# A second v piece transposed by DMA instead of on TensorE, with later weights, a closer softmax and a lagging last chunk

## The chip, the cores and the metric

The kernel runs on one core of one Trainium2 chip. The metric is the device time of one execution in microseconds. Runs agree to some 0.3%, so what is at stake here, a microsecond in 571, lies at the edge of what times alone can show. Much of the argument is therefore read from the traces, where a gap of 0.1 us on TensorE can be seen. "Clock" below means the kernel's own agenda clock, by which the program decides at build time what is emitted between which matmuls; it starts at the first main matmul of each batch, and in the first batch it is about 37.3 us behind the span's time.

In the profiles PE is TensorE (matmuls), ACT ScalarE and DVE VectorE (casts, products, copies), POOL GpSimd (it issues the loads), SP SyncE (it issues the DMA transposes and most stores); a "q" behind an engine's name is its instruction queue. A DMA "lands" when its data are all there. Batches and, by number, chunks and pieces count from 0: the second v piece of batch 0 is piece 1 in the code.

## The reference, cut to what matters

```python
# attention over channels, B, N, C = 4, 5824, 256
qn = q / (norm(q, axis=1) + 1e-6);  kn = k / (norm(k, axis=1) + 1e-6)
a = softmax(kn.transpose(0, 2, 1) @ qn / tau)          # one 256 x 256 matrix per batch
x = (v @ a).reshape(B * N, C)                          # 23296 tokens
# feed-forward, d_ff = 1024
out = ((x @ w1) * (x @ w2)) @ w3 @ w_out
```

The kernel folds the small matrix `a` into `w1` and `w2` once per batch (the folds), and `w3 @ w_out` into one matrix once for all (the w units). What is left per batch is v, transposed, times two folded weights (`a` and `b` in the profile), their product (`abs`), and that times the folded output weight (`o`).

## The kernel before

A batch has 12 chunks of 8 steps. A step is four 512-column matmuls for `a` and `b`, then a cast on ACT and a product on DVE; the output matmuls of earlier products follow. The twelfth chunk is short (192 columns). Beside batch b, the scores and the softmax of batch b + 1 run. The moves, that is, the loads, have times on the clock, and two brakes on GpSimd's queue: a `gate` copies one element of the latest product, so a load does not start early; a `hold` copies one element of a transposed v piece, so the loads behind it start only when that transpose has landed.

```python
def gate():
    if last_ab[0] is not None:
        nc.gpsimd.tensor_copy(gate_t, last_ab[0][:1, :1])
def hold(src):
    nc.gpsimd.tensor_copy(gate_t, src)
...                                                    # (cut) first batch
    moves = [("qk", 1, 0, 29.0), ("v", 0, 3, 30.0), ("v", 0, 4, 30.5), ("qk", 1, 1, 44.0), ("qk", 1, 2, 45.0)]
    moves += [("qk", 1, 3, 53.0), ("qk", 1, 4, 55.0), ("v", 0, 5, 61.0), ("qk", 1, 5, 73.0)]
    moves += [("v", 1, 0, 88.0), ("v", 1, 1, 98.0), ("v", 1, 2, 120.0), ("qk", 2, 0, 130.0)]
    t0, t1 = 54.0, 113.0                               # window of batch 1's scores
...
before = (0, 2) if b == 0 else None
for nm, m, pi, t in moves:
    if before is not None and not (nm == "v" and before == (m, pi - 1) == (0, 3)):
        at(t, 0.0, hold of the transposed piece `before`)         # (shortened)
    at(t, 0.0, gate)
    if nm == "qk":
        at(t, 0.0, lambda m=m, pi=pi: load_qk(m, pi))
        before = None                                  # behind a q/k load no hold
    else:
        at(t, 0.0, lambda m=m, pi=pi: load_piece("v", m, pi))
        at(t + 4.0, 0.0, lambda m=m, pi=pi: transpose_piece(m, pi))   # DMA transpose, SP's queue
        before = (m, pi)
```

The outputs pass through three buffers (`o_sb`, copied by ACT and DVE from PSUM, the memory that matmuls write to).

## Time and profile before

| | |
|---|---|
| time, median of all six runs taken beside the changed kernel | 571.32 us (570.57 to 572.03) |
| span of the profiled run | 569.5 us |
| first main matmul, last matmul start | 37.26, 565.36 us |
| from the last matmul's start to the end | 4.10 us |
| TensorE busy | 558.9 us (98%) |

The main lines of this profile are shown in the prediction below. Three more views matter later. The first is GpSimd's timeline, with start, duration, what it does, and in brackets the idle time before it and what ended it:

```profile
101.84 0.52 POOL L109 DMA_DIRECT2D v<-in_v_dram  x1 [0.27 <-issue]
123.52 0.18 POOL L469 COPY gate_t<-vTt 1x1 bf16<-1x1 bf16 x1 [20.60 <-DMA vTt<-v]
125.87 0.56 POOL L112 DMA_DIRECT2D k<-in_k_dram  x1
```

The sixth v piece is issued at 101.84, the hold for its transposes ends at 123.52, and the last k of batch 1 goes out behind that, at 125.87. It landed at 134.3 us. TensorE at the end of batch 2, with batch 3's exponentials in progress:

```profile
428.13 0.60 PE L519 MATMUL o<-W_sb,abs 128*128 128x256 bf16 x4
428.78 0.59 PE L477 MATMUL a<-vT,Wf 128*128 128x512 bf16 x2
```

Four 256-column matmuls need 0.44 us from start to start; here it is 0.65.

### The profile page before, as it was taken

How to read it: one execution, taken by the hardware profiler on the slowest of the kernel's cores; microseconds unless marked ns; L12 is line 12 of the kernel's file. 1: busy time of each engine (PE TensorE's matmuls, PEld its weight loads, DVE VectorE, ACT ScalarE, POOL GpSimd, SP SyncE). 2: the span in 40 equal slices, each digit the busy share in tenths (PEclk: the TensorE clock that was granted, in tenths of full speed). 3: DMA queues.
4: the chain of work that ended last, by engine and by line, in shares of the span. 5: the costliest groups of instructions: out<-in, count | busy, mean ns of one | idle time of the engine just before them, and what ended most of it. 6: DMA issues, size and time to landing. Idle time of an engine off the chain costs nothing.

```text
span 569.5 us, 10098 instructions
## 1 busy us (share of the span) xinstructions
PE 558.9 (98%) x3755; PEld 354.9 (62%) x3755; DVE 375.7 (66%) x581; ACT 340.5 (60%) x627; POOL 77.2 (14%) x163
## 2 busy tenths in 40 slices
PE   8799999999999999999999999999999999999997
PEld 5664576776666666666666666666665656656665
DVE  1047645788966577887766567787866665565564
ACT  1057535777766577777675567777756554454453
POOL 4260013020220110121210111030120000000000
PEclk9999999999999999999999999999999999999999
DMA  9999989978455696595761495766740325221011
GB/s 213 211 175 208 168 170 233 225 171 195 112 147 120 132 194 147 98 184 128 148 148 73 95 217 121 155 120 121 184 112 39 85 74 148 63 70 68 38 73 58
DMA packets 75105, 77.45 MB, mean 136 GB/s; under 512 B 54193, under 2 KB 58801, under 8 KB 75057
## 3 DMA queue, kind: packets, MB, share of 16 engines
q0 software_dynamic: 15760, 38.93, 39.1%
q1 hardware_dynamic: 59072, 37.69, 22.3%
q8 instruction: 29, 0.48, 0.3%
q10 hardware_dynamic: 224, 0.20, 0.1%
q14 instruction: 20, 0.16, 0.1%
HBM read 78.91 MB, written 23.86 MB: 180 GB/s over the span
## 4 chain that ended last, share of the span: by engine, by line
PE 91%; DMA 6%; ACT 1%; DVE 1%; POOL 0%; issue 0%; ACTq 0%; POOLq 0%
PE o L519 28%; PE b L477 27%; PE a L477 27%; PE G L193 5%; DMA k<-in_k_dram 5%; PE fold L364 2%; DMA w3T<-w_wout 1%; PE w L643 1%; ACT kr L284 0%; ACT as L483 0%; PE quarter L390 0%; POOL k L112 0%; DVE s L318 0%; ACT e L323 0%; DVE abs L498 0%
## 5 line engine op out<-in xcount | busy, mean ns | idle before, releaser
L498 DVE TENSOR_TENSOR abs<-as,b 128x512 bf16<-128x512 bf16 x336 | 230.2, 686 | 138.0 <-ACT as L483 124.9
L483 ACT CAST as<-a 128x512 bf16<-128x512 f32 (+1 forms) x384 | 216.2, 563 | 173.4 <-DVE abs L498 87.1
L477 PEld LDWEIGHTS <-Wf 128*128 128x128 bf16 x1536 | 148.8, 98 | 101.7 <-issue 1.8
L477 PE MATMUL a<-vT,Wf 128*128 128x512 bf16 x704 | 209.4, 379 | 0.4 <-ACT Wf L399 0.4
L477 PE MATMUL b<-vT,Wf 128*128 128x512 bf16 x704 | 209.4, 379 | 0.0
L519 PE MATMUL o<-W_sb,abs 128*128 128x256 bf16 x1344 | 201.1, 273 | 0.0
L519 PEld LDWEIGHTS <-abs 128*128 128x128 bf16 x1344 | 131.4, 98 | 80.8
L202 DVE TENSOR_TENSOR acc<-acc,sq 128x1024 f32<-128x1024 f32 x66 | 80.4, 1219 | 0.7 <-ACT sq L190 0.7
L193 PE MATMUL G<-k,q 128*128 128x256 bf16 x276 | 49.6, 273 | 0.0
L190 ACT ACTIVATE sq<-q 128x512 f32<-128x512 bf16 x66 | 41.8, 634 | 0.0
L190 ACT ACTIVATE sq<-k 128x512 f32<-128x512 bf16 x66 | 41.6, 630 | 0.0
L465 POOL COPY gate_t<-abs 1x1 bf16<-1x1 bf16 x39 | 9.4, 241 | 170.1 <-DVE abs L498 168.8
L540 DVE COPY osb<-o 128x512 f32<-128x512 f32 x44 | 30.1, 684 | 0.9 <-PE o L519 0.9
L193 PEld LDWEIGHTS <-q 128*128 128x128 bf16 x276 | 27.0, 98 | 3.1
L539 ACT COPY osb<-o 128x512 f32<-128x512 f32 x44 | 25.8, 586 | 3.8 <-PE o L519 1.8
L469 POOL COPY gate_t<-vT 1x1 bf16<-1x1 bf16 x16 | 3.3, 208 | 162.5 <-DMA vT<-v 162.5
L112 POOL DMA_DIRECT2D q<-in_q_dram x28 | 15.1, 539 | 12.5 <-DMA k<-in_k_dram 5.5
L284 ACT ACTIVATE kr<-row 128x256 f32<-128x256 f32 x1 | 0.4, 384 | 26.0 <-PE row L272 26.0
L371 ACT ACTIVATE Wf<-fold,rs 128x512 bf16<-128x512 f32 x15 | 10.3, 688 | 9.0 <-PE fold L364 9.0
L488 DVE TENSOR_TENSOR left<-as,b 128x192 bf16<-128x192 bf16 x32 | 11.2, 353 | 5.7 <-ACT as L483 3.5
L364 PE MATMUL fold<-w,e 128*128 128x512 bf16 x56 | 14.7, 379 | 0.0
L498 DVE TENSOR_TENSOR abq<-as,b 128x512 bf16<-128x512 bf16 x16 | 10.8, 686 | 5.1 <-ACT as L483 4.6
(98 smaller groups left out, 241.8 us busy)
## 6 DMA issues: line engine op xcount, KB each, us to landing
out_dram<-osb SPq DMA_DIRECT2D x44, 512.0 KB, 3.6
k<-in_k_dram POOLq DMA_DIRECT2D x19, 512.0 KB, 8.6
v<-in_v_dram POOLq DMA_DIRECT2D x19, 512.0 KB, 5.2
q<-in_q_dram POOLq DMA_DIRECT2D x18, 512.0 KB, 6.6
w_wout<-in_moe_w_dram POOLq DMA_DIRECT2D x1, 2048.0 KB, 23.1
k<-in_k_dram POOLq DMA_DIRECT2D x4, 320.0 KB, 7.6
v<-in_v_dram POOLq DMA_DIRECT2D x4, 320.0 KB, 5.3
q<-in_q_dram POOLq DMA_DIRECT2D x3, 320.0 KB, 4.3
```

The lines of the kernel that those rows point to most:

```text
L112: nc.gpsimd.dma_start(out=pieces[nm, n, pi][:, lo:hi, :], in_=qk_main[nm, n][0][:, pi * PIECE + lo : pi * PIECE + hi, :])
L190: nc.scalar.activation(out=dst[:, :, part, :], in_=src[:, o : o + 2, :], func=AF.Square)
L193: nc.tensor.matmul(G[:, ct, :], lhsT=qt[:, i, ct * P : (ct + 1) * P], rhs=kt[:, i, :], start=(pr == 0 and part == 0 and ct == 0), stop=(pr ...
L202: nc.vector.tensor_add(accs[n], accs[n], sqs[0])
L364: nc.tensor.matmul(m, lhsT=st["e"][:, c2, c1 * P : (c1 + 1) * P], rhs=w12[:, c2, w, lo:hi], start=(c2 == 0), stop=(c2 == CT - 1),)
L477: nc.tensor.matmul(t[:, :n], lhsT=Wf[b][:, ct, w, j * P : (j + 1) * P], rhs=rhs_of(b, c, ct), start=(ct == 0), stop=(ct == CT - 1),)
L483: nc.scalar.copy(a_sb[:, :n], tiles[0][:, :n])
L488: nc.vector.tensor_mul(both, a_sb[:, :n], tiles[1][:, :n])
L498: nc.vector.tensor_mul(ab, a_sb, tiles[1])
L519: nc.tensor.matmul(tl[h][:, o, :], lhsT=lhsT, rhs=W_sb[:, j, :], start=(j == 0 and o == 0), stop=(j == FT - 1 and (small or o == 1)), skip ...
L539: nc.scalar.copy(o[:, 0:2, :], tl[0])
L540: nc.vector.tensor_copy(o[:, 2:4, :], tl[1])
```

## The change

Its intent: sixteen PE transposes less on the bounding engine, by sending the second v piece through the DMA transpose; w3 and w_out out of its way; fewer waits at batch ends and at the program's end.

```diff
-            [(0.0, 0.0, norms), (0.0, 6.0, k_row)]
-            + [(0.0, 6.0 + 1.3 * i, lambda i=i: k_step(i)) for i in range(4)]
... (softmax units, each with closer times)
-            + [(0.2, 16.5, sums)]
-            + [(0.43, 17.5 + 1.1 * i, lambda i=i: fold(i)) for i in range(8)]
+            [(0.0, 0.0, norms), (0.0, 5.5, k_row)]
+            + [(0.0, 5.5 + 1.2 * i, lambda i=i: k_step(i)) for i in range(4)]
+            + [(0.2, 14.6, sums)]
+            + [(0.43, 15.6 + 1.1 * i, lambda i=i: fold(i)) for i in range(8)]
...
-            at(7.0, 0.5, lambda: transpose_half_on_pe(0, 1, 0, True))
-            at(8.0, 0.5, lambda: transpose_half_on_pe(0, 1, 1, False))
-            at(15.0, 0.0, transpose_w3)
-            at(15.0, 0.0, lambda: transpose_piece(0, 2))
+            at(0.0, 0.0, lambda: transpose_piece(0, 2))
+            at(0.0, 0.0, lambda: transpose_piece(0, 1))
+            at(0.0, 0.0, lambda: hold(vTs[0][0][:1, PIECE, 0, :1]))
+            at(0.0, 0.0, load_w3)
+            at(16.0, 0.0, transpose_w3)
-                at(26.0 + 1.2 * jt, 0.87, lambda jt=jt: w_unit(jt))
-            moves = [... as above ...]
+                at(35.0 + 1.2 * jt, 0.87, lambda jt=jt: w_unit(jt))
+            moves = [("qk", 1, 0, 35.0), ("v", 0, 3, 35.5), ("qk", 1, 1, 49.0), ("qk", 1, 2, 51.0), ("qk", 1, 3, 55.0)]
+            moves += [("v", 0, 4, 58.0), ("qk", 1, 4, 68.0), ("v", 0, 5, 69.0), ("qk", 1, 5, 84.0)]
+            moves += [("v", 1, 0, 92.0), ("v", 1, 1, 102.0), ("v", 1, 2, 120.0), ("qk", 2, 0, 130.0)]
+            t0, t1 = 55.0, 113.5
-        before = (0, 2) if b == 0 else None
+        before = "w3" if b == 0 else None      # hold for the last w3 transpose
...
-                lag = LAG_END if b == B - 1 and c == NCH - 1 else LAG
+                lag = LAG
+                if b == B - 1 and c >= NCH - 2:
+                    lag = LAG_END if c == NCH - 1 else LAG + (LAG_END - LAG) * (j + 1) // FT
-    while pend:
-        emit_out(*pend.pop(0))
+    n = len(pend)
+    for i, only in [(i, 1) for i in range(n - 1)] + [(i, 0) for i in range(n - 2)] + [(n - 1, 1), (n - 2, 0), (n - 1, 0)]:
+        emit_out(*pend[i], only=only)
```

In the last lines `only=1` are the leftover rows of a batch pair, `only=0` the last ordinary rows. The two stores of the leftover rows now both leave from SP; before, one left from SP and one from ACT.

More of the change, by code (lines that the diff above doesn't have):

```diff
@@ L419, in soft_units @@
         return (
-            [(0.0, 0.0, norms), (0.0, 6.0, k_row)]
-            + [(0.0, 6.0 + 1.3 * i, lambda i=i: k_step(i)) for i in range(4)]
-            + [(0.0, 6.5, q_sums), (0.0, 9.3, lambda: q_norm(st["ss"]))]
-            + [(0.0, 11.3 + 1.3 * ct, lambda ct=ct: scale(ct)) for ct in range(CT)]
-            + [(0.0, 12.0 + 1.3 * ct, lambda ct=ct: exps(ct)) for ct in range(CT)]
-            + [(0.2, 16.5, sums)]
-            + [(0.43, 17.5 + 1.1 * i, lambda i=i: fold(i)) for i in range(8)]
+            [(0.0, 0.0, norms), (0.0, 5.5, k_row)]
+            + [(0.0, 5.5 + 1.2 * i, lambda i=i: k_step(i)) for i in range(4)]
+            + [(0.0, 6.0, q_sums), (0.0, 8.5, lambda: q_norm(st["ss"]))]
+            + [(0.0, 10.3 + 1.2 * ct, lambda ct=ct: scale(ct)) for ct in range(CT)]
+            + [(0.0, 11.0 + 1.2 * ct, lambda ct=ct: exps(ct)) for ct in range(CT)]
+            + [(0.2, 14.6, sums)]
+            + [(0.43, 15.6 + 1.1 * i, lambda i=i: fold(i)) for i in range(8)]
         )
@@ L501, in emit_ab, with emit_out @@
         clock[0] += 4 * (n * MM_COL + MM_FIX)
-    def emit_out(b, c, j, ab):
+    def emit_out(b, c, j, ab, only=None):
         small = c == NCH - 1
@@ L517, in emit_out @@
         for s, lhsT in reversed(list(enumerate(lhs))) if small else enumerate(lhs):
+            if only is not None and s != only:
+                continue
             h, o = (s, 0) if small else divmod(s, 2)
@@ L528, in emit_out @@
             if small:
-                nc.scalar.copy(o[:, 0, :], tl[0][:, 0, :])
-                other = nc.scalar if b == B - 1 else nc.sync
-                other.dma_start(out=rows[:, NT - 1, :], in_=o[:, 0, :])
-                if b % 2 == 1:
+                if b % 2 == 1 and only != 0:
                     o2 = work.tile([P, D], F32, tag="kr", name=f"oleft_{b}", bufs=1)
                     nc.vector.tensor_copy(o2, tl[1][:, 0, :])
-                    for k, eng in enumerate((nc.sync, other)):
-                        m = b - 1 + k
-                        eng.dma_start(out=out[m * N + NT * P : (m + 1) * N, :], in_=o2[k * LEFT : (k + 1) * LEFT, :])
+                    for m in (b - 1, b):
+                        k = (m - b + 1) * LEFT
+                        nc.sync.dma_start(out=out[m * N + NT * P : (m + 1) * N, :], in_=o2[k : k + LEFT, :])
+                if only != 1:
+                    nc.scalar.copy(o[:, 0, :], tl[0][:, 0, :])
+                    other = nc.scalar if b == B - 1 else nc.sync
+                    other.dma_start(out=rows[:, NT - 1, :], in_=o[:, 0, :])
             else:
@@ L541, in emit_out @@
                 nc.sync.dma_start(out=rows[:, 4 * c : 4 * c + 4, :], in_=o)
-            del out_tiles[b, c]
+            if only is None:
+                del out_tiles[b, c]
     NDEF = 4
@@ L615 @@
     load_piece("v", 0, 2)
-    nc.gpsimd.dma_start(out=wout_sb, in_=moe_w_out.rearrange("(lh ll) c -> ll lh c", ll=P))
-    nc.gpsimd.dma_start(out=w3_bf, in_=w3r)
     squares("k", 4, whole)
@@ L652, in w_unit, with load_w3 @@
             w_ready[0] = True
+    def load_w3():
+        nc.gpsimd.dma_start(out=wout_sb, in_=moe_w_out.rearrange("(lh ll) c -> ll lh c", ll=P))
+        nc.gpsimd.dma_start(out=w3_bf, in_=w3r)
     def load_library():
@@ L669, in make_agenda @@
             at(4.6, 0.5, lambda: transpose_half_on_pe(0, 0, 1, False))
-            at(7.0, 0.5, lambda: transpose_half_on_pe(0, 1, 0, True))
-            at(8.0, 0.5, lambda: transpose_half_on_pe(0, 1, 1, False))
-            at(15.0, 0.0, transpose_w3)
-            at(15.0, 0.0, lambda: transpose_piece(0, 2))
-            for jt in range(FT):
-                at(26.0 + 1.2 * jt, 0.87, lambda jt=jt: w_unit(jt))
-            moves = [("qk", 1, 0, 29.0), ("v", 0, 3, 30.0), ("v", 0, 4, 30.5), ("qk", 1, 1, 44.0), ("qk", 1, 2, 45.0)]
-            moves += [("qk", 1, 3, 53.0), ("qk", 1, 4, 55.0), ("v", 0, 5, 61.0), ("qk", 1, 5, 73.0)]
-            moves += [("v", 1, 0, 88.0), ("v", 1, 1, 98.0), ("v", 1, 2, 120.0), ("qk", 2, 0, 130.0)]
-            t0, t1 = 54.0, 113.0
+            at(0.0, 0.0, lambda: transpose_piece(0, 2))
[3 more added lines that the diff above has]
+            at(16.0, 0.0, transpose_w3)
+            for jt in range(FT):
+                at(35.0 + 1.2 * jt, 0.87, lambda jt=jt: w_unit(jt))
[3 more added lines that the diff above has]
+            t0, t1 = 55.0, 113.5
         else:
@@ L685, in make_agenda @@
             t0, t1 = 16.0, 98.0
-        before = (0, 2) if b == 0 else None
+        before = "w3" if b == 0 else None
         for nm, m, pi, t in moves:
             if before is not None and not (nm == "v" and before == (m, pi - 1) == (0, 3)):
-                at(t, 0.0, lambda w=before: hold(vTs[w[0]][1][:1, 0, :1] if w[1] == NP_ - 1 else vTs[w[0]][0][:1, w[1] * PIECE, 0, :1]))
+                at(t, 0.0, lambda w=before: hold(w3T[-1][:1, 1, FT - 1, :1] if w == "w3" else vTs[w[0]][1][:1, 0, :1] if w[1] == NP_ - 1 else vTs[w[0]][0][:1, w[1] * PIECE, 0, :1]))
             at(t, 0.0, gate)
```

## The prediction

> **What bounds the kernel now.** I read the page's busy shares first, then the chain, then who waited on TensorE, then TensorE's timeline at the four places that the diff touches.
>
> ```profile
> span 569.5 us, 10098 instructions
> PE 558.9 (98%) x3755; PEld 354.9 (62%) x3755; DVE 375.7 (66%) x581; ACT 340.5 (60%) x627; POOL 77.2 (14%) x163
> PE   8799999999999999999999999999999999999997
> DMA  9999989978455696595761495766740325221011
> PE 91%; DMA 6%; ACT 1%; DVE 1%; POOL 0%; issue 0%; ACTq 0%; POOLq 0%
> ```
>
> TensorE is busy in every slice after the second, and the chain lies on it for 91%. DMA is full only in the first fifth. A busy PE need not run at its peak, because ends are modelled. So I took the distance from each matmul's start to the next: the median is 216 ns for 512 columns, 109 ns for 256, 82 ns for 192, 56 ns for 128. From 37.3 us (the first main matmul) to the last start at 565.4 us only some 3.3 us lie above these medians. So nothing beside TensorE can win more than that there; the rest must come from fewer matmuls or from the two ends. Where the 3.3 us are:
>
> ```profile
> 63.56 0.59 PE L477 MATMUL b<-vT,Wf 128*128 128x512 bf16 x2
> 64.28 1.05 PE L643 MATMUL w<-w_wout,w3T 128*128 128x256 bf16 x8
> ...
> 67.33 0.59 PE L477 MATMUL b<-vT,Wf 128*128 128x512 bf16 x2
> 68.21 1.92 PE L643 MATMUL w<-w_wout,w3T 128*128 128x256 bf16 x16 [0.29 <-DMA w3T<-w_wout]
> ```
> The step from 63.56 to 64.28 is 0.72 us where two 512-column matmuls need 0.43: 0.29 lost. The second is 0.88 for 0.43: 0.45 lost. Both wait for w3's transposes; 0.74 us in all.
>
> ```profile
> 178.38 0.33 PE L477 MATMUL a<-vTt,Wf 128*128 128x192 bf16 x2
> 178.68 0.33 PE L477 MATMUL b<-vTt,Wf 128*128 128x192 bf16 x2
> 178.84 0.27 PE L519 MATMUL o<-W_sb,left 128*128 128x256 bf16 x1
> 179.12 0.33 PE L477 MATMUL a<-vTt,Wf 128*128 128x192 bf16 x2
> 179.54 0.33 PE L477 MATMUL b<-vTt,Wf 128*128 128x192 bf16 x2
> ```
> Two 192-column matmuls need 0.16; here 0.30 and 0.42. The short last chunk of a batch meets the folds' evictions on ACT and DVE. By the same reading the four batch ends lose 0.74, 0.18, 0.47 (of it 0.26 beside the exponentials at 428 us) and 0.62 us.
>
> ```profile
> 559.93 0.33 PE L477 MATMUL a<-vTt,Wf 128*128 128x192 bf16 x2
> 560.29 0.33 PE L477 MATMUL b<-vTt,Wf 128*128 128x192 bf16 x2
> ...
> 564.15 1.47 PE L519 MATMUL o<-W_sb,left 128*128 128x256 bf16 x12
> 565.66 0.37 ACT L529 COPY osb<-o 128x256 f32<-128x256 f32 x1 [1.16 <-PE o L519]
> 566.07 0.41 ACTq L531 DMA_DIRECT2D out_dram<-osb  x1
> 566.52 0.53 ACTq L537 DMA_DIRECT2D out_dram<-oleft  x1
> ```
> In the very last chunk the first four pieces come with no output matmul between them, so TensorE runs ahead of ACT and DVE. After the last matmul come a copy, two DMA issues one behind the other on ACT's queue, and the landing: its record is at 568.5, the span ends at 569.5.
>
> **What the Trainium skill says.** "TensorE: Matmul & The Clock Gate", section "Wait — 56ns, not 53.3ns?", gives a warm start-to-start time of columns / 2.4 GHz + about 2.5 ns, 55.6 ns for 128 and 215.7 for 512; the trace agrees (56 and 216), so TensorE is already at its pace. The same page, Part 4, has about 275 ns for one PE transpose in a kernel's context. This trace differs: each is modelled at 219 ns, but eight in a row take 0.45 us on the path, 56 ns each. I use 56. "DMA: Bandwidth & Descriptors", section "Latency and other measured facts", gives a DMA transpose 261 GB/s. A piece here is 524 KB, so an estimate from that page is 2.0 us; back-to-back ones landed at 69.98, 71.98 and 73.91 us, so the trace agrees. The same page, "Rules for kernel authors", says that a transpose beside ordinary DMAs needs nothing; all here leave SP, one stream, so no new wait is forced.
>
> **The change part by part.**
>
> 1. *Second v piece.* It removes two halves of 8 PE transposes each: 16 x 56 ns = 0.90 us, straight off the path. With them go the wait of the first of them for its v piece (0.11 us at 44.8; the piece landed at 44.77) and two evictions (ACT 1.01 us, DVE 0.69 us) that were beside other work. In their place are DMA transposes, issued as third piece, then second. The third landed at 47.2 us; from issue to landing 3.6 us is the median and the next lands 2.0 behind: about 51 and 53 us. The second piece is wanted by chunk 2, which started at 55.36 and will start 1.0 us earlier, at 54.35. A margin of 1.3 us, so free if the first transposes are not slow. But the first w3 transposes were: 4.4 us to land and the second 3.9 us behind. With that the second piece lands at 55.5, a wait of 1.2. I count 0.4.
>
> 2. *w3 and w_out behind that.* They were issued at 35.8 and 36.7 us behind v and landed at 49.9 and 59.8; from v's end to w3's, 12.5 us for 2.62 MB, or 209 GB/s. Now they wait on a GpSimd hold until the second piece is transposed: issue at about 53.3, first bytes some 2.6 us later (a lone 512 KB load landed 5.1 us after issue, of it 2.5 for the bytes), end at 68.4. The transposes then land at 72 to 73 (first) and 79 to 81 (fourth). The w units move from 26 to 35 on the kernel's clock, so the first is wanted near 72.6 us, the second near 75.2, the third 77.8, the last 80.4. That fits within a microsecond either way: I leave the wait of 0.74 as it is, estimate 0 to 2. Deferred products rise from some 31 to 41; 16 lie in q's buffers and there are 34 more, so they fit.
>
> 3. *q, k and v loads later.* They now wait for the last w3 transpose (80 us; before 74). v piece 3 lands near 91 and its transpose near 95; chunk 6 wants it near 95 to 96 us (seven steps of 1.73 us after the last w unit). Before, the slack was over 10 us. The q and k of batch 1, pieces 1 to 3, go out near 95 and their scores start piece 1 near 104 us; k lands at 103. Both without a wait by this count, with 1 us to spare. I add 0.2. The later move of the fifth v piece behind q and k has over 10 us of slack.
>
> 4. *Closer softmax.* No matmul goes. Batches 1 and 2: the folds come 1.9 us earlier and end before the short chunk. Batch 0: the score window ends 0.5 later and two transposes (1.0) have left the clock, so relative to the work the folds move by only 0.4 us. The all-reduce (3.23 us) ended 2.0 us before ACT wanted it in batch 1 and 0.5 us before in batch 0; asking half a microsecond sooner costs nothing or next to nothing. Of 1.4 us at three batch ends I expect 0.4 back.
>
> 5. *Lagging last outputs.* The lag grows over chunk 10, so its outputs stand between the short pieces of the last chunk. The three waits there (0.19, 0.05, 0.20: 0.44) go; the 0.18 at 562.9 stays, since it is the third output buffer that waits for the copy of chunk 10.
>
> 6. *The last drain.* Ten matmuls as before, but the leftover rows finish two matmuls earlier (0.22 us), and their two DMAs leave from SP while ACT's copy and DMA go alone. SP's second issue would start near 566.3 instead of ACT's at 566.5, landing about 2.0 later: 0.2 us.
>
> Sum: -0.90 - 0.11 + 0.4 + 0 + 0.2 - 0.4 - 0.44 - 0.2 = -1.45 us. From 571.08: 569.6.
>
> **The rivals.** *A wait for data takes the place of the transposes.* For it: steps 1 to 3 all have about 1 us of slack in a stretch where DMA shows 9 in nearly every slice, and the earlier w3 transposes had a stutter of 2 us between the first and second. Against it: the holds leave the transposes alone on the engines, and the loads are spaced to the microsecond, which looks tuned. If each is late by 1 to 1.5 us, the time is 571 to 573. *All waits go* (w3 in time, batch ends clean): w3's 0.74 and a further 0.6 are won, and step 1's 0.4 and step 3's 0.2 not lost: 567.7. *Only the end is won*, the transposes being free anyway because TensorE waits for w3 later: about 570.3. *ACT or DVE become the bound*: they are at 60% and 66% and lose work, so no.
>
> **Range and chances.** The three runs of before spread over 1.5 us. The middle is 569.6; 568.0 to 571.8 takes in the all-waits-go end and one late transfer. Over 2% faster would need 11.4 us, where removed work and all waits are near 4.5; over 2% slower needs a load late by a whole piece or a stall behind a hold. So same 0.97, slower 0.02, faster 0.01.
>
> **What would show it.** In the changed profile TensorE has 16 matmuls fewer and one 0.45 us group of transposes instead of three after the start. At chunk 2 (near 54.4 us) either no gap or a wait for the DMA of vT. At the w groups (72 to 82 us) the waits for w3T, under 2 us in sum. At chunk 6 (95 us) a gap only if step 3 is wrong. At 178, 428 and 444 us shorter gaps; at 560 us steps of 0.16 us after each short piece; SP, not ACT, issuing the last DMA. The prediction is wrong if a wait of over 2 us stands at one of the first three, or if the exponentials, now closer, hold up ACT's evictions.

## More of the kernel before

Where "granted clock" is said, the share of TensorE's full speed is meant that the trace shows as granted.

SP issues the transposes and the output stores in one order.

What SP waited for after 565 us (in total, times, longest, us):

```profile
SPq L755 <- DMA out_dram<-osb: 1.0, 1, 1.0
SPq L755 <- DMA out_dram<-oleft: 0.4, 1, 0.4
```

These are the waits for the last stores, at the closing of the program.

## The result, and the profile after

| | before | changed |
|---|---|---|
| median of six runs each | 571.32 us | 571.78 us (571.27 to 573.77) |
| ratio, 95% interval | | 1.0011 (0.9995 to 1.0028) |
| span of the profiled run | 569.5 us | 569.8 us |
| first main matmul to last matmul start | 528.10 us | 527.58 us |
| last matmul start to the end | 4.10 us | 4.73 us |

Ratios in this text are the mean time of one kernel's fast runs over that of the other's fast runs of the same rounds, so they are not quite the ratio of the medians. This one is "same", and the promised microsecond and a half is not there.

The page and the chain of the changed kernel:

```profile
span 569.8 us, 10067 instructions
PE 557.2 (98%) x3739; PEld 354.4 (62%) x3739; DVE 375.3 (66%) x580; ACT 339.0 (60%) x626; POOL 78.7 (14%) x165
PE 80%; DMA 15%; POOL 2%; issue 1%; ACT 1%; DVE 0%; SPq 0%; POOLq 0%; ACTq 0%
```

Sixteen matmuls fewer, and TensorE 1.7 us less busy, in a span that is no shorter. The chain has moved off TensorE: DMA 6% became 15%. The reader should ask at once which DMA. TensorE's timeline, first at the w units, then at 144 us:

```profile
72.13 0.59 PE L477 MATMUL b<-vT,Wf 128*128 128x512 bf16 x2
72.57 1.04 PE L646 MATMUL w<-w_wout,w3T 128*128 128x256 bf16 x8
...
143.83 0.60 PE L522 MATMUL o<-W_sb,abs 128*128 128x256 bf16 x4
146.35 0.60 PE L193 MATMUL G<-k,q 128*128 128x256 bf16 x4 [1.92 <-DMA k<-in_k_dram]
```

At 72 us the step is 0.44, as it should be: the wait for w3 is gone here. At 143.83 four matmuls that need 0.44 us take 2.52, so 2.09 us are lost: the scores of batch 1 wait for their last k. GpSimd's timeline tells why k is late:

```profile
99.39 0.53 POOL L112 DMA_DIRECT2D v<-in_v_dram  x1
121.19 0.18 POOL L469 COPY gate_t<-vT 1x1 bf16<-1x1 bf16 x1 [21.27 <-DMA vT<-v]
123.59 0.57 POOL L112 DMA_DIRECT2D v<-in_v_dram  x1
135.70 0.18 POOL L469 COPY gate_t<-vTt 1x1 bf16<-1x1 bf16 x1 [11.54 <-DMA vTt<-v]
138.05 0.56 POOL L112 DMA_DIRECT2D k<-in_k_dram  x1
```

Two holds stand one behind the other. The fifth v piece is now loaded behind three pairs of q and k, lands at 117.3 and is transposed at 121.1. Only then may the fifth q and k and the sixth v piece go; that one is transposed at 136. Only then may the last q and k go. The last k leaves 12 us later than before, lands at 146.31 us, and was due at 144.3.

The end of the program:

```profile
560.14 0.33 PE L477 MATMUL b<-vTt,Wf 128*128 128x192 bf16 x2
560.30 0.60 PE L522 MATMUL o<-W_sb,abs 128*128 128x256 bf16 x4
...
563.88 1.47 PE L522 MATMUL o<-W_sb,left 128*128 128x256 bf16 x12
565.38 0.37 ACT L539 COPY osb<-o 128x256 f32<-128x256 f32 x1 [1.16 <-PE o L522]
565.62 1.12 SPq L537 DMA_DIRECT2D out_dram<-oleft  x2
565.79 0.38 ACTq L541 DMA_DIRECT2D out_dram<-osb  x1
```

Outputs now stand between the short pieces, each of which takes its 0.16 us. But SP's waits after 565 us read

```profile
SPq L767 <- DMA out_dram<-oleft: 1.6, 1, 1.6
```

and the last landing, at 568.45 us, is followed by 1.35 us until the end of the span, where before it was 0.92 us (568.53 to 569.46).

From these numbers the whole difference of the two profiled runs adds up. Above TensorE's median steps: transposes -0.90, waits at 44 and 54 us -0.25, w3 -0.74, exponentials at 428 us -0.26, last chunk -0.44; together -2.59 us. Against it +2.09 at 144 us. That is -0.50, and the matmul window is 0.52 us shorter. The start of the first main matmul is 0.24 later, in a stretch whose work the change leaves alone but for two load issues at its end (over all profiled runs it lies between 36.9 and 37.8 us). The tail is 0.63 longer. -0.52 + 0.24 + 0.63 = +0.35 us, which is the difference of the spans.

The terms of this sum are not independent. What was won ahead of 144 us (0.90 + 0.25 + 0.74 = 1.89 us) made TensorE arrive earlier at a k that lands when its chain of loads and holds lets it; had nothing been won there and k landed at the same time, the wait would have been some 0.2 us (an estimate from these figures). Run 4 below shows it: TensorE lost 0.71 us to w3 there, k landed at 146.32 us as here, and the wait was 1.57 us instead of 2.09. So the late k cost the changed kernel nearly all that its front had won.

### The profile page after: what moved, and what is told of

It is laid out like the page before. It is cut to its first block, busy times and chain, and to the rows that moved or that the text cites. A ratio compares the mean times of both kernels' runs of the same rounds, so it can differ in the third digit from the quotient of the medians.

```text
span 569.8 us, 10067 instructions
## 1 busy us (share of the span) xinstructions
PE 557.2 (98%) x3739; PEld 354.4 (62%) x3739; DVE 375.3 (66%) x580; ACT 339.0 (60%) x626; POOL 78.7 (14%) x165
## 4 chain that ended last, share of the span: by engine, by line
PE 80%; DMA 15%; POOL 2%; issue 1%; ACT 1%; DVE 0%; SPq 0%; POOLq 0%; ACTq 0%
PE b L477 25%; PE a L477 25%; PE o L522 23%; DMA v<-in_v_dram 6%; DMA k<-in_k_dram 4%; PE G L193 4%; PE fold L364 2%; DMA q<-in_q_dram 2%; DMA vT<-v 1%; POOL q L112 1%; POOL k L112 1%; DMA w3T<-w_wout 1%; DMA vTt<-v 1%; ACT kr L284 0%; POOL gate_t L465 0%
## 5 line engine op out<-in xcount | busy, mean ns | idle before, releaser
L112 POOL DMA_DIRECT2D v<-in_v_dram x25 | 13.5, 542 | 4.2 <-issue 3.2
```

The source lines that it names most:

```text
L112: nc.gpsimd.dma_start(out=pieces[nm, n, pi][:, lo:hi, :], in_=qk_main[nm, n][0][:, pi * PIECE + lo : pi * PIECE + hi, :])
```

## The experiments

Twelve kernels ran, all correct; each has one trace. Gaps are worked out as in the prediction: start-to-start time of TensorE's matmuls over the median for their size. A step that is too long by just 0.21 us and that nothing ended is a matmul record missing from the trace, and is not counted. (The 0.21 us at 428 us in the kernel before is not of that kind: its trace has all 3755 records, as many as weight loads, and in run 4 and run 7 the same step is long.)

**1. Without the hold ahead of the last q and k.**

```diff
-            if before is not None and not (nm == "v" and before == ...):
+            if before is not None and before != (0, 5) and not (nm == "v" and before == ...):
```

> The changed kernel without the one GpSimd hold that makes the last q and k of batch 1 wait for the transposes of the sixth v piece; order and clock times of the loads stay. Theory A (chain of holds): q and k go out near 124 us instead of 136.5, k lands near 135 instead of 146.3, the 2.09 us gap of TensorE at 144 us is gone, and the time falls by 2.1 us, to about 569.7. Theory B (the loads' bandwidth is what is late): k lands near 144 or later all the same, at least 1 us of the gap stays, time 571 or more.

The last k landed at 135.55 us, as theory A had it, and the gap at 144 us was gone. Yet five of six runs took 579 to 581 us, and one took 571.23; the kernel before took 570.28 to 571.06 on the same chip in eleven runs. The ratio 1.0079 (1.0025 to 1.0134) is from one run of each kind, so it says little. The trace of one of the five shows that the time is lost in the kernel's own waits, and the mean granted clock of the other four (0.988 to 0.991, as its 0.991) fits the same event; why the sixth run escaped it is not known.

```profile
142.09 0.38 PE L522 MATMUL o<-W_sb,abs 128*128 128x256 bf16 x2
151.02 0.58 PE L522 MATMUL o<-W_sb,abs 128*128 128x256 bf16 x2 [8.54 <-ACT osb L543]
151.40 1.06 PE L193 MATMUL G<-k,q 128*128 128x256 bf16 x4
```

An output matmul waits 8.7 us for ACT to free its PSUM tile, and for some 4 us after that each matmul takes twice its time: the granted clock in the trace was 0.5 from 145.06 to 155.30 us. ACT waited for an output buffer, whose store, issued at 136.0 us behind the sixth v piece's three transposes, landed only at 150.3. The transposes were issued at 131.6 to 134.3 us and landed at 147.5 to 147.9. With the hold gone, the gate alone let batch 1's first v piece go out at 131.90 us, and it too landed at 147.3. The view by stretches of time, from 134 to 147 us (busy time of PE, PEld, DVE, ACT and POOL, then clock, DMA share and GB/s):

```profile
134.00:147.00 13.00, 8.47 (x63) 5.93 (x61) 7.06 (x8) 5.10 (x10) 0.00 (x0) 0.93 1.23 79
```

The time that the DMA packets took adds up to 1.23 of the engines' time, so there were transfers in flight throughout, and they moved 79 GB/s. So theory A was right on the hold and wrong on the time: the hold also kept a load away from the transposes, and that was worth more than it cost (that it was this load, run 8 tests).

**2. The last q and k ordered ahead of the sixth v piece; the hold stays.**

```diff
-  ("v", 0, 4, 58.0), ("qk", 1, 4, 68.0), ("v", 0, 5, 69.0), ("qk", 1, 5, 84.0)
+  ("v", 0, 4, 58.0), ("qk", 1, 4, 68.0), ("qk", 1, 5, 69.0), ("v", 0, 5, 70.0)
```

> The changed kernel with the last q and k of batch 1 ordered ahead of the sixth v piece; the hold stays, but now stands in front of batch 1's first v piece. Theory A: no gap at 144 us, q and k land near 133 us, the sixth v piece is transposed near 139 us and is wanted only near 163; time as without the hold, about 569.7. Theory B: the gap stays at 1 us or more.

The last k landed at 133.1 us and the gap at 144 us was gone. But 570.92 us, ratio 1.0004 (0.999 to 1.0019): a new gap of 1.06 us.

```profile
141.53 0.38 PE L522 MATMUL o<-W_sb,abs 128*128 128x256 bf16 x2
142.81 0.38 PE L522 MATMUL o<-W_sb,abs 128*128 128x256 bf16 x2 [0.90 <-ACT osb L543]
```

SP's timeline in this run shows what ACT waited for:

```profile
119.02 0.52 SPq L545 DMA_DIRECT2D out_dram<-osb  x1
134.88 1.24 SPq L161 DMA_TRANSPOSE vT<-v  x1
139.32 1.76 SPq L545 DMA_DIRECT2D out_dram<-osb  x3
```

SP stands at the transpose from 119.5 until the v piece lands at 134.86, and three stores pile up behind it: all three output buffers. In the changed kernel the same three stores went out at 135.3 to 137 us, just in time.

**3. The fifth v piece straight behind the fourth again.** Only the moves of the first batch differ: `("v", 0, 3, 35.5), ("v", 0, 4, 36.0)`, then q and k 1 to 4, then v 5.

> The changed kernel with the fifth v piece loaded straight behind the fourth again, as before the change; all else as changed. If this part of the change was needed because w3 now comes later: the hold for the fifth v piece sends q and k of batch 1 out near 100 us instead of 94.9, k lands near 107.5 and TensorE waits some 3 us for it near 104 us; sixth pieces come earlier, so the gap at 144 us is gone or small. If the part is neutral: no gap at 104 us and the time 2 us under the changed kernel.

The first expectation held: a gap of 2.54 us at 102.6 us, where the second pieces of q and k are late, and none at 144 us. One run: 571.75 us. So with w3 coming later this part of the change is not free to undo; it traded a wait of 2.5 us at 102 us for one of 2.1 us at 144 us.

**4. The softmax spaced as before.** The list of softmax times is that of the kernel before.

> The changed kernel with the softmax spaced as before. If the closer spacing is what took away the waits near 428 us: they come back, 0.26 us in sum; the four other batch-end waits stay within 0.1 us of the changed kernel's; the gap at 144 us stays 2.1 us. If the spacing is neutral: no wait over 0.1 us near 428. In both, time within 0.4 us of the changed kernel, not to be told apart by the time.

The waits near 428 us came back, 0.27 us in sum. The first line below is of this run, its step 0.65 instead of 0.44:

```profile
428.45 0.60 PE L522 MATMUL o<-W_sb,abs 128*128 128x256 bf16 x4
429.10 0.59 PE L477 MATMUL a<-vT,Wf 128*128 128x512 bf16 x2
```

The end of batch 0 lost 0.88 us against 0.74 in the changed kernel and 0.74 before, a little over the 0.1 allowed; the other batch ends stayed. So the closer softmax is worth a quarter of a microsecond on TensorE: the three traces with the old spacing have this wait, the eleven with the new one do not. The time of the one run, 571.76 us, can't show it. The expectation for 144 us missed: the gap was 1.57 us and not 2.1, because TensorE came 0.5 us later to a k that landed at the same time. The wait for w3 was 0.71 us in this run: the first w3 transpose landed at 73.0 us and not at 72.4. That wait depends on when w3 lands in a run. Over the twelve profiled kernels with the changed front it was nothing in four, two of which ask for w3 a step later, 0.26 to 0.71 us in seven, and 1.65 us in one. The kernel before varies too: 0.74 us in its own trace, 0.30 in that of run 7, which has its front.

**5. The swap, with the sixth piece's transposes issued later.** They stand at 100 on the clock, behind two more stores, and batch 1's first v pieces at 101 and 109.

```diff
-                at(t + 4.0, 0.0, lambda m=m, pi=pi: transpose_piece(m, pi))
+                at(t + (30.0 if (m, pi) == (0, 5) else 4.0), 0.0, lambda m=m, pi=pi: transpose_piece(m, pi))
```

> As the swap run (last q and k of batch 1 ahead of the sixth v piece), and the sixth piece's transposes are issued from SP 30 us later on the clock, with batch 1's first v pieces behind them. Theory: the 1.06 us gap that the swap run had at 141.6 us came from output stores standing behind those transposes in SP's order, which filled the three output buffers. Then no gap over 0.2 us is left between 85 and 165 us, and the time is about 1 us under the swap run and 2 us under the changed kernel: 569.8. Rival (the gap is the stores' own bandwidth): a gap of about 1 us stays near 141 us.

Between 85 and 165 us no gap is left. SP issues the stores as they come, ahead of the transposes:

```profile
118.82 14.71 SPq L545 DMA_DIRECT2D out_dram<-osb  x4
137.37 2.15 SPq L161 DMA_TRANSPOSE vT<-v  x1
```

569.59 us, ratio 0.9989 (0.9975 to 1.0003). The interval just takes in no difference from the kernel before, so the time alone does not decide. The gaps settle the middle of the kernel: the chain of holds made k late, and the order on SP was the next limit behind it.

**6. The changed kernel with seven more store issues.** Seven output stores of batch 2 are split in two.

> The changed kernel with seven more DMA issues: seven output stores of batch 2 split in two. Nothing else moves. Theory C (SP ends by passing its DMA semaphores in a fixed order, and the last store of the changed kernel lies early in it, so that the later ones are passed one by one after it): eight semaphores take turns, so seven issues more put the last store back at the end of the order; from the last matmul's start to the end of the span 4.3 us instead of 4.73, from the last landing to the end 0.9 instead of 1.35. Rival (the last landing alone decides): 4.7 and 1.35 stay.

The tail from the last matmul's start fell to 4.29 us, and from the last landing to the end to 0.92, as theory C had it. SP's waits after 565 us:

```profile
SPq L771 <- DMA out_dram<-oleft: 0.8, 1, 0.8
SPq L771 <- DMA out_dram<-osb: 0.3, 1, 0.3
```

DMAs from SP and ACT take eight semaphores in turn. At the end SP passes them in a fixed order, one every 0.06 us. The kernel before makes 88 such DMAs, eleven full turns, so its last store has the last semaphore. The changed kernel makes 89, because the second v piece is one transpose more; its last store has the first of the eight, and seven passes come behind it: 7 x 0.06 = 0.43 us, which was the difference. Seven more issues make 96 and give it back. Every trace with the new order of the last stores agrees: the tail is 4.71 to 4.73 us in the seven kernels with 89 such DMAs, and 4.27 to 4.29 us in the four with 88 or 96. The time of the one run was 571.02 us.

**7. The kernel before with the lag and the last drain alone.** `emit_out`, the lag and the last loop are those of the change.

> The kernel before with the lag and the last drain of the change alone; its number of DMA issues is that of before. The three waits at 560 us (0.44 us) go, the 0.18 one stays; with theory C the tail from the last matmul's start to the end is 4.1 us or less (before 4.10), not 4.73, as the issues are a multiple of eight; time 0.4 to 0.6 us under before. Rival: if the new order of the last stores itself lengthened the tail, it is 4.7 us and the time is the same as before.

The three waits at 560 us were gone, the 0.18 stayed. The tail was 4.27 us, between the two expectations: not 4.73, as the semaphore order is that of before, but not under 4.10 either. From the last matmul's start to the last landing it took 3.37 us, as in the changed kernel and in run 6; the kernel before took 3.18. So the new order of the stores costs 0.19 us where I had counted a gain. SP's second store was issued 0.08 us sooner after the last matmul than ACT's was, but landed 2.29 us after its issue instead of 2.01. Why is open. Time 570.35 us, ratio 0.9996 (0.9984 to 1.0009): the 0.25 us that the two parts leave (0.44 - 0.19) is less than these times can resolve.

**8. Without the hold, but batch 1's first v piece later.** Run 1, with that load at 101 instead of 92 on the clock, and the next v piece at 109 instead of 102.

> As the run without the hold, but the first v piece of batch 1 is loaded 9 us later on the clock, so that it no longer goes out beside the sixth v piece's transposes. If that load and the transposes held each other up (both landed at 147 us there): the transposes land by 139 us, no gap of 8.7 us and no halved clock, time about 570. If the tail of q and k beside the transposes is enough: the gap stays over 4 us and the time over 575.

The three transposes landed by 136.96 us, no gap in this stretch, no halved clock. 569.59 us (two runs), ratio 0.9980 (0.9963 to 0.9997). The same stretch as in run 1:

```profile
134.00:147.00 13.00, 13.00 (x98) 9.37 (x96) 11.21 (x14) 9.74 (x18) 1.51 (x2) 1.00 0.88 249
```

249 GB/s instead of 79. The last k landed at 134.78, still beside the transposes' first part. So it was the 512 KB load issued right behind the first transpose that crawled with them.

**9 and 10. Three additions to runs 5 and 8:** the two leftover stores as one DMA, the w units from 35.9 on the clock, the scores' window ended at 112.0.

```diff
-                        nc.sync.dma_start(out=out[m * N + NT * P : (m + 1) * N, :], in_=o2[k : k + LEFT, :])
+                    both = out.rearrange("(m n) c -> m n c", n=N)[b - 1 : b + 1, NT * P :, :]
+                    nc.sync.dma_start(out=both, in_=o2)
```

> A version meant to beat both: the swap with late transposes, and besides: the two leftover stores of a batch pair as one DMA (two issues fewer in all, one fewer at the end), the first w unit one step later, and batch 0's score window ended at 112.0 instead of 113.5 on the clock, so that its folds are done ahead of the short chunk. Expected against the swap with late transposes: the wait for w3 at 72 us (0.27) goes, of the 0.74 at 177 us at least half goes, the tail from the last matmul's start to the end falls from 4.72 to about 4.2 us; 1.1 us less in all, near 568.5. If the folds' place is not what makes batch 0's end wait, the 0.74 stays. If one DMA in place of two lands no sooner, the tail is 4.3 or more.

> The same three additions on the version without the hold and with the later first v piece of batch 1. Expected the same time, near 568.5; this one tells whether the version without the hold now and then falls into the slow crawl of loads beside transposes (570 and above in some runs) that five of six runs without the hold showed. If it is safe: all runs within 1.5 us.

A miss: 572.34 and 571.81 us, ratios 1.0020 (1.0006 to 1.0034) and 1.0014 (1.0001 to 1.0026), where 568.5 was expected. The wait for w3 went and batch 0's end fell from 0.74 to 0.22 us, as expected. But k was late by 0.44 and 1.02 us near 102 us, output copies near 158 and 165 us cost 0.84 and 0.44, and the one DMA for both stores made the tail 7.08 and 7.12 us:

```profile
SPq L766 <- DMA out_dram<-oleft: 4.5, 1, 4.5
```

Here I should have looked before I built. The Trainium skill's page "DMA: Bandwidth & Descriptors", section "Rules for kernel authors", says that an outermost dimension below 16 confines a DMA to at most that many engines. My destination began with a dimension of two. The trace fits: in run 9 the store was issued at 564.2 and landed at 569.65 us, and in the raw trace its semaphore rose three times, against 16 times for each of the other last stores. With two stores again, run 11's tail is 4.29 us. Run 10's five runs lie within 1.04 us and run 8's two within 0.81, so in these seven runs the version without the hold is steady, with no load going out beside the transposes.

**11 and 12. Run 5 with the seven split stores of run 6;** in 12 also the scores' window from 57.0 to 112.5.

> The swap with late transposes, and seven more store issues of batch 2 split in two, so that the last store again has the last semaphore in SP's final order. The leftover stores stay two (one DMA for both landed 5.5 us after its issue in the last two runs). Expected: tail from the last matmul's start to the end 4.3 us instead of 4.72, no gap over 0.35 us from 45 to 165 us, time 0.4 under the swap with late transposes: about 569.2, faster than both kernels by 0.2 to 0.4%.

> The same with batch 0's score window from 57.0 to 112.5 on the clock instead of 55.0 to 113.5. Expected: the 0.74 at batch 0's end falls to 0.3 or less, and no wait for k near 102 us, as the scores start 2 us later; if the softmax chain then collides with the output copies near 158 or 165 us as in the last two runs, 0.4 to 0.8 comes back and the time is that of the other run.

569.53 us, ratio 0.9977 (0.9963 to 0.9990), and 569.37 us, ratio 0.9969 (0.9956 to 0.9983). Both beat the kernel before and, by their medians on other chips, the changed kernel by some 2.3 us. The tails were 4.29 and 4.27 us. Run 11 waited 0.46 us for w3, over the 0.35 expected. In run 12 batch 0's end cost 0.21 us instead of 0.74 and nothing collided near 158 or 165. Its profiled run (570.25, the slowest of five) waited 1.65 us for w3, whose transposes landed 1.7 us later than in the changed kernel's profile; its fastest took 568.55. That wait may be what still varies; with one trace for each kernel this is not shown.

## Why the prediction was wrong

The time was off by 2.2 us and the sign with it: -1.45 was expected, +0.46 between the medians was measured (the interval reaches from -0.3 to +1.6 us). That the miss is 2.2 and not 1.9 us is only because I counted from 571.08. Point by point:

- *Step 1* was right and its surcharge not needed. The second v piece was transposed at 52.4 us (predicted 53) and wanted at 54.4; 0.90 + 0.25 us were won on TensorE and none of the 0.4 paid. Of the 0.25 I had counted 0.11; the 0.14 us at 54.6 us I had not seen, and run 7, which has the front of the kernel before, shows that wait again (0.13) but not the 0.11.
- *Step 2* was right in its times: w3 landed at 68.5 (68.4 predicted), its transposes at 72.4 to 78.4. In the profiled run even the 0.74 went, which is luck of the run: in seven other traces a wait of 0.26 to 0.71 us stays, and in one of 1.65.
- *Step 3* is the step that failed, in its last sentence: "The later move of the fifth v piece behind q and k has over 10 us of slack." That was true of the fifth v piece and its own chunk. I did not follow what else stands behind it. Its transpose ends a hold, behind that comes the sixth v piece, whose transposes end the next hold, and behind that the last q and k, which came 2.1 us too late for TensorE. The slack of the list is that of its last item. Runs 2, 5 and 8 remove that wait in two ways, and it goes each time. Under the rivals I had written that the holds leave the transposes alone on the engines; that much was right (run 1), but I took it as a reason against a wait, and the holds were what made it. The other figures of the step held: the fourth v piece transposed at 94.0 (95 predicted), the second k landed at 102.5 (103).
- *Step 4* was mis-sized: 0.26 us was won of the 0.4 expected, all at 428 us; batch 0's end kept its 0.74. With the old spacing (run 4) the 0.26 us is lost again.
- *Step 5* was right to the hundredth: 0.44 went, 0.18 stayed.
- *Step 6* had the wrong sign: -0.2 was expected, +0.63 measured. 0.19 of it is the later landing of the last store (run 7), 0.43 the place of its semaphore in SP's closing order (run 6), of which I knew nothing.
- Two readings were loose, and nothing rests on them: the gaps above the medians add up to 3.2 us and not 3.3, and DMA shows 9 also in three single slices behind the first fifth.

Of the rivals, "a wait for data takes the place of the transposes" came closest to what happened, but not where it was sought: none of the three places named for it waited in the profiled run, and the wait stood at 144 us, two holds further on. With step 3's wait removed and the 0.43 of step 6 given back, the change comes to about what was expected of it: run 11 is 1.3 us under the kernel before, by its ratio. Run 12, at 1.8 us, has the shorter scores' window besides, which is no part of the change.

## What to carry to other kernels

When loads are chained by waits, follow the chain to its last item and compare that one's landing with its due time; a comfortable slack in the middle says nothing. What is won ahead of such a late item is lost again in waiting for it. Before taking a wait away, ask what else it keeps apart: this hold cost 2 us, and without it five of six runs lost some 9. And on a kernel whose bound engine is 98% busy, add up start-to-start times and the two ends separately; a gain of half a microsecond can be undone by how many DMAs the program issues.

## What the Trainium skill lacked or had wrong

- "DMA: Bandwidth & Descriptors", section "Rules for kernel authors", says that a transpose next to ordinary DMAs needs nothing. That may hold for the data, but not for time: in run 1 three transposes and a 512 KB load in flight together moved 79 GB/s and took over 13 us to land; kept apart, the transposes landed in 3.2 to 5.4 us and the same stretch moved 249 GB/s (run 8).
- "TensorE: Matmul & The Clock Gate", Part 4, gives some 275 ns for a PE transpose in a kernel, and no pace for several in a row. In this trace each is shown as 219 ns long, but eight in a row took 0.45 us on the path, 56 ns each.
- No page that I read has how a kernel's own DMA semaphores are passed at its end: here SP passes the DMA semaphores in a fixed order at 0.06 us each, and the last store's place in that order was worth 0.43 us (run 6).
- Nor did I find a page that warns of transposes and stores sharing SP's order: SP stood for 15 us at a transpose that waited for its load, three output stores piled up behind it (run 2), and TensorE lost 1.06 us.
